# Attention and a mixture of experts in one program: blanking placed by the planner, a second raw buffer at the start, whole-chunk scores for the first pair, and the early expert's first layer beside the last pair

## The chip, the cores and the metric

The program runs on one core of one Trainium2 chip, in one launch. The metric is the device time of an execution in microseconds (us). The kernel before took 1047.83 us in the median of 3 runs (1040.9 to 1049.94).

## The reference

Two stages follow each other. The first is attention with a threshold, for 8 batches (B) of 8 heads (H), 576 positions (S) and 64 channels (D):

```python
scores = scale * np.matmul(q, k.transpose(0, 1, 3, 2))
thresh = np.max(scores, axis=-1, keepdims=True) - tau
scores = np.where(scores >= thresh, scores, -1000000000.0)
scores = scores - np.max(scores, axis=-1, keepdims=True)
attn = np.exp(scores)
attn = attn / (np.sum(attn, axis=-1, keepdims=True) + 1e-09)
return np.matmul(attn, v).astype(np.float32)
```

The second takes the result as 4608 tokens of 512 values and sends each token to one of 8 experts (512 to 1024 to 512):

```python
do_compute = x @ w_skip > 0                 # a token may be skipped: out = x
e_idx = np.argmax(xc @ w_gate, axis=1)      # gate_w is its softmax weight
h = np.maximum(xc[mask] @ w1[e], 0.0)
out = xc + gate_w[mask, None] * (h @ w2[e])
```

## The kernel before, in words

**Pairs and chunks.** The attention is cut into 32 pairs of heads (`g`, four to a batch). The 576 positions are four blocks of 128 and a tail of 64; the tails of a pair's two heads share one block, so a pair has nine chunks (`STEP = 9`): four for each head and one for both tails. Float32 values are split in a high part (`h`) and the rest (`l`), and products are made of the parts.

For each pair `plan_pair` loads q and k as `raw` (128 x 1152 values), casts them to the high part (`hi`, one cast on VectorE or ScalarE) and makes the rest in two halves (`lo`, one for q and one for k, on VectorE or GpSimd). `plan_dist` writes the parts by DMA into a large buffer QK (three transfers of 64 x 1152 values for each head, three buffers in a ring, pair `g` in buffer `g % 3`), and copies two rows of zeros (`zd`, in DRAM) into it; `plan_blk` fills the block BD for the tails. `plan_score` multiplies a chunk's 128 queries with all 576 keys, in two halves of 288 that each have a PSUM buffer (`shp`), and VectorE takes the maximum of each half (`mx`). Once a pair's 18 maxima are there, `plan_thresh` works out the thresholds on VectorE (`mm`, then three steps on `gps`, then `nh` in two parts), PE transposes them to rows (`plan_trow`, L667), and ScalarE puts these into QK. `plan_weights` then multiplies again, now with the threshold subtracted by the product itself (L565, PSUM `sps`), ScalarE exponentiates (`e`, L711), VectorE masks (`p`, L716), `p` is split into fp16 parts (`phh` on ScalarE or VectorE, `phl` on GpSimd, L753), and `plan_av` multiplies with v (L784). v is loaded once for a batch in four transfers of 384 KB (`plan_v`, L459).

**Experts.** After each batch the tokens' logits are computed (`plan_logits`, and `plan_tails` for the tails), `plan_gate` picks experts and slots in lists on VectorE, and GpSimd scatters records to these lists in DRAM (L1134). When seven batches are through, the fullest expert is picked and its first 256 tokens are worked on while the last pairs of the attention still run (`plan_pick`, `plan_early`: its weights are split in high and low parts, `wl` at L1278; its first layer's products are at L1331, with the hidden values in the buffers QK0 and QK1). When all slots are known, the experts' lists are loaded and sorted by size, and eight experts are worked through, of each `layer1`, then `layer2` (L1602).

**What sets the order.** Nothing of the attention is written in the order in which it runs. Each step is an operation of a plan, with the engines that may take it and an estimated cost, the operations it needs, the ring buffer it takes, and a due time: `k` or `n` counts chunks, and the table `OFF` shifts each kind of step against it. `Plan.run` walks forward in its own estimated time, and gives each engine the due operation that can start first. So a changed entry of `OFF` or a new operation moves others, and can move them to another engine. Engines that issue in this fixed order wait on semaphores; SP issues all plain loads and stores in one queue. Before the plan begins, a stretch of plain code sets up constants: GpSimd writes zeros, ones and -1 into the QK, BD, V and `nh` buffers (L274 to L294) and builds index tables, all of it ahead of its first planned operation. A warm-up of 10 products (`WARM`) runs on PE.

Of the kernel before, what the change touches and what calls it, by code (L numbers as in the profile page):

```python
# [62 lines left out]
XW = -7.2  # L63
VS = -2.6
V2 = 60.3
GS = 0.12
DU = 5
WRB = 4
LOOK = 0.1
WARM = 10  # L70
# [6 lines left out]
    ld=19.0, hl=-60.5, hlD=97.9, loD=230.0, di=17.3, S=-15.2, mx=6.5, th=-131.9, tr=-4.4, tc=-40.8, T=-11.5, e=-54.1, p=-11.3, ph=1.9, phD=16.2, pl=0.0, av=4.0, ldv=18.9, v=-11.2, v0=0.0, fmA=4.0, ld0=0.0, init=39.5, row=10.6, dh=21.2, bd=10.6, rsp=-1.6, vsp=49.0, L1=24.0, sc=0.0,  # L77
# [102 lines left out]
def attn_moe_kernel(ctx: ExitStack, tc: tile.TileContext, qk, vl, tau, wg, w1, w2, out):  # L180
# [24 lines left out]
    iod = cp.tile([P, E], F32, name="iod")
    nc.vector.tensor_scalar(iod, ioe, -1.0, float(E - 1), op0=ALU.mult, op1=ALU.add)
    capc = cp.tile([P, 2, E], F32, name="capc")
    for i, cap in enumerate(CAPS):
        nc.gpsimd.memset(capc[:, 0, i : i + 1], float(cap))
        nc.gpsimd.memset(capc[:, 1, i : i + 1], float(cap // P))  # L210
    eoff = cp.tile([P, E], F32, name="eoff")
    nc.vector.tensor_scalar(eoff, ioe, float(NTOK), None, op0=ALU.mult)
    tokp = cp.tile([P, NTP], F32, name="tokp")
    for i in range(2):
        nc.gpsimd.iota(
            tokp[:, i * NM : (i + 1) * NM],
            [[P, NM]],
            base=i * S,
            channel_multiplier=1,
            allow_small_or_imprecise_dtypes=True,  # L220
        )
# [53 lines left out]
    for i in range(QB):  # L275
# [5 lines left out]
        if i == QB - 1:  # L281
            break
# [670 lines left out]
    def plan_tails(b, k, xtm):  # L953
# [31 lines left out]
        if b == B - 1:  # L985
            plan_gate(k + 2, pr, 2 * NM, 1, [y])
# [891 lines left out]
```

## Time and profile before

| what | before |
| --- | --- |
| median of 3 runs | 1047.83 us |
| the profiled execution | 1047.14 us |
| its span (first to last instruction of the profile) | 1045.2 us |
| VectorE busy, instructions | 790.9 us, 1747 |
| TensorE (PE) busy, products | 903.1 us, 9592 |
| ScalarE (ACT) busy | 586.9 us |
| GpSimd (POOL) busy | 685.1 us |
| mean granted clock of TensorE | 0.928 |

Times in a view count from the start of the span. A row of the timeline has the start, the duration, the engine, the line of the kernel, the operation, output <- inputs, the shape, the count of instructions that it groups, and in brackets the idle time ahead of it with what ended that. A row of the groups has line, engine, operation, count, then busy time in us, mean ns of one, and the idle time of the engine before them by what ended it. A row of the windows has the stretch, then for PE, its weight loads, VectorE, ScalarE and GpSimd the busy time and instructions, then the granted clock, the share of the DMA engines and GB/s. SPq stands for DMA issues on SP. The chain that ended last has only its last operations in this profile, so the stages are read from the windows and the timeline.

### The profile page before, as it was taken

To read this page: it belongs to the slowest core of one execution; us is meant where nothing else is said; L and a number is where in the kernel's file an instruction comes from. 1 tells how busy PE (TensorE), PEld (TensorE's weight loads), DVE (VectorE), ACT (ScalarE), POOL (GpSimd) and SP (SyncE) were. 2 spreads that over 40 slices of the span, in tenths; PEclk is the share of its full clock that TensorE was granted. 3 is DMA by queue.
4 is the path that set the end of the run, shared out by engine and by line. 5 is a ranking of instruction groups with operands and counts; after the bars stand their busy time and mean duration, and the time that the engine had idled before them with its cause. 6 is when DMAs were issued, how large, how long until landed. Compare 5 with 4: busy or idle time off the path is not lost. (4 is left out here: it accounts for less than half of the span.)

```text
span 1045.2 us, 24717 instructions
## 1 busy us (share of the span) xinstructions
PE 903.1 (86%) x9592; PEld 833.4 (80%) x9592; DVE 790.9 (76%) x1747; ACT 586.9 (56%) x856; POOL 685.1 (66%) x444
## 2 busy tenths in 40 slices
PE   1888998998799898788899969885787999999995
PEld 1568887987788798688888969875786989999994
DVE  2678988899989689999879989997653455547771
ACT  0356886785577586557768647755441434434450
POOL 6338796796887678688768877957634446544561
PEclk6599999999999899989989989997788999999998
DMA  3976558649447765845865775471234655444530
GB/s 98 243 165 145 132 116 249 145 103 263 109 109 201 191 137 120 236 116 119 212 154 123 199 185 126 86 219 32 82 101 140 213 181 172 130 168 164 193 131 17
DMA packets 81814, 157.39 MB, mean 151 GB/s; under 512 B 28631, under 2 KB 28887, under 8 KB 81696
## 3 DMA queue, kind: packets, MB, share of 16 engines
q1 hardware_dynamic: 77008, 145.51, 53.0%
q0 software_dynamic: 4544, 10.28, 3.0%
q8 instruction: 77, 1.26, 0.5%
q14 instruction: 41, 0.34, 0.1%
q10 hardware_dynamic: 144, 0.00, 0.0%
HBM read 70.80 MB, written 24.78 MB: 91 GB/s over the span
## 5 line engine op out<-in xcount | busy, mean ns | idle before, releaser
L753 POOL TENSOR_TENSOR phl<-p,phh 128x1152 f16<-128x1152 f32 x128 | 310.2, 2426 | 110.3 <-ACT phh L328 89.2
L596 DVE TENSOR_REDUCE mx<-shp 128x1 f32<-128x288 f32 x576 | 245.8, 447 | 45.3 <-PE shp L591 44.0
L591 PE MATMUL shp<-QK 128*128 128x288 f32 x1024 | 225.1, 330 | 47.4 <-DVE mx L596 30.0
L711 ACT ACTIVATE e<-sps,ntau 128x576 f32<-128x576 f32 x288 | 207.1, 736 | 90.9 <-PE sps L565 75.1
L716 DVE SCALAR_TENSOR_TENSOR p<-sps,e 128x576 f32<-128x576 f32 x288 | 214.8, 749 | 36.6 <-ACT e L711 26.9
L591 PEld LDWEIGHTS shp<-QK 128*128 128x128 f32 x1024 | 163.3, 201 | 65.2 <-DVE mx L596 50.7
L565 PE MATMUL sps<-QK 128*128 128x288 f32 x1024 | 192.1, 318 | 17.9 <-DVE p L716 15.0
L565 PEld LDWEIGHTS sps<-QK 128*128 128x128 f32 x1024 | 152.9, 199 | 25.8 <-DVE p L716 18.2
L328 ACT ACTIVATE phh<-p 128x1152 f16<-128x1152 f32 x111 | 128.8, 1161 | 52.0 <-DVE p L716 32.8
L784 PE MATMUL avp<-Vh,phl 128*128 128x65 f16 x1280 | 140.4, 200 | 9.3 <-POOL phl L753 9.2
L780 PE MATMUL avp<-Vh,phh 128*128 128x65 f16 x1280 | 142.6, 202 | 0.5 <-ACT a L328 0.5
L783 PE MATMUL avp<-Vl,phh 128*128 128x64 f16 x1280 | 141.0, 199 | 0.0
L784 PEld LDWEIGHTS <-phl 128*128 128x128 f16 x1280 | 123.8, 102 | 9.9 <-POOL phl L753 9.8
L780 PEld LDWEIGHTS <-phh 128*128 128x128 f16 x1280 | 122.6, 102 | 9.2
L783 PEld LDWEIGHTS <-phh 128*128 128x128 f16 x1280 | 124.0, 103 | 0.7 <-issue 0.6
L1531 POOL TENSOR_TENSOR wl<-wr,wh 128x1024 fp32r<-128x1024 f32 x28 | 72.3, 2599 | 34.7 <-ACT wh L1530 29.4
L1568 PE MATMUL hps<-xh,wl 128*128 128x256 f32 (+4 forms) x256 | 76.7, 300 | 0.0
L1568 PE MATMUL hps<-xh,wh 128*128 128x256 f32 (+4 forms) x248 | 76.2, 307 | 0.1
L1568 PE MATMUL hps<-xl,wh 128*128 128x256 f32 (+4 forms) x248 | 74.8, 301 | 0.0
L1580 POOL DMA_INDIRECT out<-o,ids x21 | 21.1, 1003 | 71.7 <-DVE o L1579 30.1
L1569 ACT ACTIVATE QK<-hps 128x256 fp32r<-128x256 f32 (+4 forms) x64 | 27.0, 422 | 68.3 <-PE hps L1568 67.7
L381 POOL TENSOR_TENSOR hl<-raw,hl 128x576 fp32r<-128x576 f32 x31 | 44.3, 1430 | 30.6 <-ACT vmx L516 16.8
(243 smaller groups left out, 1988.7 us busy)
## 6 DMA issues: line engine op xcount, KB each, us to landing
QK<-hl SPq DMA_DIRECT2D x192, 288.0 KB
wr<-in_w SPq DMA_DIRECT2D x32, 1024.0 KB
raw<-in_qk SPq DMA_DIRECT2D x32, 576.0 KB
vraw<-in_vl SPq DMA_DIRECT2D x32, 384.0 KB
out<-xb SPq DMA_DIRECT2D x32, 256.0 KB
xs<-xb SPq DMA_DIRECT2D x32, 256.0 KB
BD<-hl SPq DMA_DIRECT2D x64, 64.0 KB
QK<-zd SPq DMA_DIRECT2D x64, 4.5 KB
```

What stands on the lines that cost most here:

```text
L328: nc.scalar.activation(dst, src, AF.Copy)
L565: nc.tensor.matmul(ps[:, j, 0:HS], w_, x_[:, js], start=(i == 0), stop=(i == len(mm) - 1))
L591: nc.tensor.matmul(ps[:, 0:HS], w_, x_[:, js], start=(q == 0), stop=(q == len(mm) - 1))
L596: nc.vector.tensor_reduce(T["mx", g][:, o, j : j + 1], T.pop(("S", g, i, j))[:, 0:HS], AX.X, ALU.max)
L711: nc.scalar.activation(e, T["W", g, i][:, :, 0:HS], AF.Exp, bias=ntau, scale=0.125)
L716: nc.vector.scalar_tensor_tensor(T[z][:, kt % 2].rearrange("p (a b) -> p a b", a=2), T.pop(("W", g, i))[:, :, 0:HS], 0.0, T.pop(("e", g, i ...
L753: nc.gpsimd.tensor_tensor(T["pl", g, i], T.pop(z)[:, 0:nk], T["ph", g, i], op=ALU.subtract)
L780: nc.tensor.matmul(pv[:, c, :], x, Vh[:, hd, kt, :], start=(j + q + c == 0), stop=False, skip_group_check=True)
L783: nc.tensor.matmul(pv[:, c, 0:D], x, Vl[:, hd, kt, :], start=False, stop=False, skip_group_check=True)
L784: nc.tensor.matmul(pv[:, c, :], y, Vh[:, hd, kt, :], start=False, stop=(c == NM), skip_group_check=True)
L1531: lo[q % 2].tensor_tensor(w[1][:, sl], rs, w[0][:, sl].bitcast(F32), op=ALU.subtract)
L1568: nc.tensor.matmul(hp_[:, 0:cap], w_, x, start=(i == 0), stop=(i == len(mm) - 1))
```

## The change

1. **The plan's numbers.** Most entries of `OFF` change, with `XW`, `VS`, `V2` and `DU`; the plan's estimate for a DMA of QK rises from 0.82 to 1.08, for a load of raw from 1.64 to 2.17 and of v from 1.1 to 1.44. `WARM` goes from 10 to 24.
2. **Blanking.** Of the plain code ahead of the plan only what pair 0 and pair 1 need is left: VectorE blanks QK1, GpSimd writes its rows of -1, BD0, `nh`, `jt`, then QK2 and BD1. The rest (`settle_a` to `settle_e`: the ones in V, the blanks of QK0, the tables, `seg`) become operations of the plan, due later. Pair `g` now uses QK buffer `(g + 1) % 3`. The copies of zero rows into QK are made only from the fourth pair on, and `zd` is filled later, from a small tile of its own.
3. **Loads at the start.** Pair 1's raw values have a buffer of their own (in the ring `xb`), so their load no longer waits for pair 0's parts. The first loads of v now wait until SP has issued the second head's transfers of pair 0.
4. **Whole chunks.** The scores of pair 0 go into a whole `sps` buffer, and VectorE takes both halves' maxima of a chunk in one instruction.
5. **The early expert.** Its second half of w1 has a buffer in `xb`. Its transposes and first-layer products use the `shp` buffers in place of `sps`, and the buffers QK0 and QK1, which the last pair no longer occupies.
6. **One last gate.** For the last batch, tails and main tokens are transposed into `sps` buffers one after the other, and one gate of five columns takes the place of two gates with one and four.

```diff
+    for h in range(2):
+        blank_qk(nc.vector, 1, h)
+        minus_qk(1, h)
+    nc.gpsimd.memset(BDs[0].bitcast(F32), 0.0)
+    nc.gpsimd.memset(nhs[0].bitcast(F32), 0.0)
...
-        QK, BD = QKs[g % QB], BDs[g % 2]
+        QK, BD = QKs[(g + 1) % QB], BDs[g % 2]
...
+            if g == 1:
+                T["raw", g] = ap_.tile([P, 2 * S], F32, name="raw1", tag="xb")
...
-        mine = [pl.dma(k - OFF["di"] + OFF["dh"] * h - 0.1, zero, ring.take(f"QK{h}", QB), [0.05])]
+        mine = [pl.dma(kd - 0.1, zero, qr + [T["init"]], [0.05])] if g >= QB else []
...
+        def both():
+            T["S", g, i, 0] = ps = sps()
+            for j in range(2):
+                score(j, ps[:, j])
...
+            nc.vector.tensor_reduce(T["mx", g][:, o, :], T.pop(("S", g, i, 0))[:, :, 0:HS], AX.X, ALU.max)
...
-            if b >= B - 2:
-                plan_gate(k + 2, pr, (b % 2) * NM, NM, [y])
+            elif last:
+                plan_gate(k + 2, pr, NM, NM + 1, [y, T["lgt", pr]])
...
-        if b == B - 1:
-            plan_gate(k + 2, pr, 2 * NM, 1, [y])
...
-        x = pl.op(k2, xt, gs + ring.take("sps", SPB), {PE: 0.108 * NDT * jt})
+            t = pl.op(k2 + a, lambda a=a: xt(a), gs + ring.take("shp", SHB), {PE: 0.108 * 2 * jt})
...
+    settle = [
+        pl.op(-40, settle_a, T["start"][1], {DVE: 1.6}),
+        pl.op(62, settle_c, T["start"][1], {POOL: 1.3}),
+        pl.op(64, lambda: settle_b(0), T["start"][1], {POOL: 1.7}),
+        pl.op(65, lambda: settle_b(1), T["start"][1], {POOL: 1.7}),
+        pl.op(70, settle_d, T["start"][1], {POOL: 1.4}),
+    ]
```

What the new numbers and operations do to the order is seen on three queues. A number behind a name tells buffers apart. First SP, from its first load on; `in_qk` and `in_vl` are the inputs in DRAM. Before, where QK_156 is pair 0's buffer:

```order
L360 DMA raw<-in_qk 128x1152
L297 DMA zd<-nh_185 128x9 [waits Pool_49]
L427 DMA QK_156<-zd 2x576 [waits DMAHW2_49]
...
L459 DMA vraw<-in_vl 128x768
...
L1419 TENSOR_LOAD tneg [waits DVE_49]
...
L436 DMA QK_156<-hl 64x2x576 [waits DMAHW5_49,DVE_49]
L438 DMA QK_156<-hl 64x1152 [waits DMAHW6_49,DVE_49]
L440 DMA QK_156<-hl 64x2x576 [waits DMAHW7_49,Pool_49]
...
L360 DMA raw<-in_qk 128x1152 [waits DMAHW2_49]
```

Now, where QK_115 is pair 0's buffer and raw_191 the buffer of pair 1:

```order
L382 DMA raw<-in_qk 128x1152
L1475 TENSOR_LOAD tneg [waits DVE_49]
...
L382 DMA raw_191<-in_qk 128x1152
L461 DMA QK_115<-hl 64x2x576 [waits DVE_49]
L463 DMA QK_115<-hl 64x1152 [waits DVE_49]
L465 DMA QK_115<-hl 64x2x576 [waits Pool_49]
...
L484 DMA vraw<-in_vl 128x768 [waits DMAHW1_49]
...
L437 DMA BD_117<-hl 64x4x64 [waits DMAHW5_49]
...
L461 DMA QK_116<-hl 64x2x576 [waits DMAHW7_49,Activation_49]
...
L382 DMA raw<-in_qk 128x1152 [waits DMAHW2_49]
```

The zero rows and the four loads of v stood ahead of pair 0's parts and now stand elsewhere or behind; pair 1's load moved ahead of them, and the last row, the load of pair 2, stands behind v, BD and half of pair 1's parts.

Second VectorE, from the last maximum of pair 0 to the end of its thresholds (`mm` to `nh`). Before:

```order
L624 TENSOR_REDUCE mm<-mx 128x9 [waits DVE_49]
L628 TENSOR_SCALAR gps<-mm 128x9 [waits DVE_49,Activation_49]
L596 TENSOR_REDUCE mx<-shp 128x1 [waits PE_49]
L632 SCALAR_TENSOR_TENSOR gps<-mm,gps 128x9 [waits DVE_49]
...
L636 SCALAR_TENSOR_TENSOR gps<-mm,tau_123,gps 128x9 [waits DVE_49]
...
L644 CAST nh_185<-gps 128x5 [waits DVE_49,Pool_49]
```

Now:

```order
L668 TENSOR_REDUCE mm<-mx 128x9 [waits DVE_49]
...
L622 TENSOR_REDUCE mx<-shp 128x1 [waits PE_49] x2
L348 CAST hl<-raw 128x2x576 [waits DMAHW2_49]
L672 TENSOR_SCALAR gps<-mm 128x9 [waits Activation_49]
L622 TENSOR_REDUCE mx<-shp 128x1 [waits PE_49]
L676 SCALAR_TENSOR_TENSOR gps<-mm,gps 128x9 [waits DVE_49]
```

The cast of pair 2's high part (L348), which waits for its raw load, now stands between the first and the second link of pair 0's threshold chain.

Third PE, at the end of the attention; `x` and `xb` are the last batch's tails and main tokens, `wgt` the gate's weights, and `tri` the product in each gate that ranks tokens. Before:

```order
L887 MATMUL gps<-ident,x_10811 128x128 x4
...
L1331 MATMUL sps<-QK_156,wl_12898 128x256
...
L1075 MATMUL gps<-rs_13241,tri_74 128x8
...
L887 MATMUL gps<-ident,xb 128x128 x4
L912 MATMUL gps<-wgt,xf 128x16 x4
L1075 LDWEIGHTS tri_74
L1075 MATMUL gps<-rs_13327,tri_74 128x8
...
L1602 MATMUL yps<-wh,QK_156 128x512
```

Now:

```order
L1387 MATMUL shp<-QK_114,wl_12610 128x256
L929 MATMUL sps<-ident,x_10699 128x128 x4
L929 MATMUL sps<-ident,xb 128x128 x4
L1018 MATMUL sps<-wgt,xf 128x16 x2
L955 MATMUL sps<-wgt,xf 128x16 x2
...
L1120 MATMUL gps<-rs_13281,tri_140 128x8
...
L1668 MATMUL yps<-wh,QK_114 128x512
```

The two gates have become one, with both transposes directly ahead of it. Before, 84 of the first layer's 96 products stood behind the last product of the attention; now 36 do, and 48 more than before stand ahead of it.

More of the change, by code (lines that the diff above doesn't have):

```diff
@@ L398, in plan_pair @@
         ]
-        ring.free("raw", [a] + c)
+        ring.free("xb" if g == 1 else "raw", [a] + c)
         T["lo", g] = c
@@ L468, in plan_v @@
                     lambda i=i: load(i),
-                    [(y,) for y in lds[-1:]] or ring.take("vraw", 1) + ring.take("V", 2) + T["start"][0],
-                    [1.1],
+                    [(y,) for y in lds[-1:]] or ring.take("vraw", 1) + ring.take("V", 2) + T["start"][1],
+                    [1.44],
                     0.46,
@@ L598, in plan_score, with tops @@
         deps = [T["bd", g]] if M else T["qk", g, h]
-        for j in range(2):
+        wide = g == 0
+        def both():
+            T["S", g, i, 0] = ps = sps()
+            for j in range(2):
+                score(j, ps[:, j])
+        def tops():
+            if i == 0:
+                T["mx", g] = ap_.tile([P, STEP, 2], F32, name="mx", tag="mx")
+            nc.vector.tensor_reduce(T["mx", g][:, o, :], T.pop(("S", g, i, 0))[:, :, 0:HS], AX.X, ALU.max)
+        if wide:
+            s = pl.op(n + OFF["S"], both, deps + ring.take("sps", SPB), {PE: 0.86 if M else 0.57})
+            m = pl.op(n + OFF["mx"], tops, [s] + (ring.take("mx", 2) if i == 0 else T["mxo", g][0:1]), {DVE: 0.75})
+            ring.free("sps", [m])
+            T.setdefault(("Sop", g, h), []).append(s)
+            T.setdefault(("mxo", g), []).append(m)
+        for j in range(0 if wide else 2):
             s = pl.op(
@@ L891, in ev @@
             copy(e, xf, T.pop(("X", key)))
-        t = pl.op(k, tr, deps + ring.take("gps", 1), {PE: 0.434})
+        t = pl.op(k, tr, deps + (ring.take("sps", SPB) if last else ring.take("gps", 1)), {PE: 0.434})
         x = pl.op(k + 0.3, ev, [t] + ring.take("xf", 2), {ACT: 0.478})
-        ring.free("gps", [x])
+        if not last:
+            ring.free("gps", [x])
         return t, x
@@ L983, in plan_tails @@
         T["lgt", pr] = y = pl.op(k + 1.8, lg, js + [T["lgo", b - 1]], {DVE: 0.1})
-        ring.free("gps", [y])
-        if b == B - 1:
-            plan_gate(k + 2, pr, 2 * NM, 1, [y])
+        ring.free("sps" if last else "gps", [y])
     cnt_op = []
@@ L1110, in plan_gate @@
         gs = GS if pr < B // 2 - 1 else 0.5
-        o = pl.op(k, alloc, deps + ring.take("gate", 2), {DVE: 0.1})
+        o = pl.op(k, alloc, deps + T["settle"] + ring.take("gate", 2), {DVE: 0.1})
         o = x = pl.op(k + gs, a1_, [o] + ring.take("ca", 1), {DVE: 0.2})
@@ L1147, in plan_gate @@
         ring.free("gate", scs)
[L1148 removed]
+        if t0 + nt == NTP:
             ring.free("lg", [o])
@@ L1338, in plan_early @@
                         mm,
-                        [x] + hs + ls + (ring.take("sps", SPB) if i == 0 else mms),
+                        xo[-2:] + hs + ls + (ring.take("shp", SHB) if i == 0 else mms),
                         {PE: 12 * 0.109},
@@ L1358, in plan_early @@
             y = pl.op(k2 + 1.7 + f2, hl, [y], {DVE: 0.66})
-            ring.free("sps", [y])
+            ring.free("shp", [y])
             T.setdefault("L1", []).append(y)
```

284 lines of the change are left out of this document (154 added, 130 removed).

## The prediction

> **What bounds the kernel now.** I read the page first (span, engine shares, slices), then the windows of the first 50 us and the timeline there, then the timeline from 715 us to 803 us, and last the groups of instructions between 60 and 700 us. The page:
>
> ```profile
> span 1045.2 us, 24717 instructions
> PE 903.1 (86%) x9592; PEld 833.4 (80%) x9592; DVE 790.9 (76%) x1747; ACT 586.9 (56%) x856; POOL 685.1 (66%) x444
> DVE  2678988899989689999879989997653455547771
> ```
>
> The span lies 1.94 us under its execution (1047.14 us), which is 0.7 us under the median of the runs shown (1047.83 us); I sum against 1047.14. VectorE's slices (tenths, 26 us each) run at eight and nine for most of the attention, but the first three, 2, 6 and 7, are thin: there the kernel waits for a chain, not for an engine. The windows, whose last column is what the DMA engines moved in GB/s, and the timeline of the start:
>
> ```profile
> 20.00:25.00 5.00, 0.00 (x0) 0.00 (x0) 1.75 (x1) 0.00 (x0) 0.00 (x0) 0.50 0.97 340
> 25.00:30.00 5.00, 0.95 (x2) 0.36 (x2) 2.47 (x5) 0.00 (x0) 0.00 (x0) 0.50 1.06 204
> 30.00:35.00 5.00, 4.79 (x15) 3.71 (x15) 3.04 (x8) 2.09 (x4) 0.84 (x1) 0.50 1.00 255
> 35.00:40.00 5.00, 3.46 (x11) 2.55 (x11) 3.75 (x7) 4.96 (x4) 1.91 (x2) 0.50 1.16 236
> 40.00:45.00 5.00, 4.86 (x18) 3.81 (x16) 3.02 (x7) 0.00 (x0) 4.64 (x2) 0.50 0.97 238
> ```
>
> ```profile
> 0.74 0.40 SPq L360 DMA_DIRECT2D raw<-in_qk  x1
> ...
> 2.54 1.05 POOL L278 MEMSET QK<- 64x1152 f32 x1
> ...
> 3.93 0.57 POOL L279 MEMSET QK<- 2x576 f32 x1
> ...
> 5.45 0.52 POOL L284 MEMSET BD<- 128x512 f32 x1
> ...
> 7.45 0.76 DVE L381 TENSOR_TENSOR hl<-raw,hl 128x576 fp32r<-128x576 f32 x1
> ...
> 15.88 1.40 POOL L381 TENSOR_TENSOR hl<-raw,hl 128x576 fp32r<-128x576 f32 x1
> ...
> 18.93 1.79 SPq L459 DMA_DIRECT2D vraw<-in_vl  x4
> ...
> 23.45 0.96 SPq L440 DMA_DIRECT2D QK<-hl  x1
> ...
> 30.07 2.46 PE L591 MATMUL shp<-QK 128*128 128x288 f32 x7 [0.50 <-DMA QK<-hl]
> ...
> 43.81 0.46 DVE L596 TENSOR_REDUCE mx<-shp 128x1 f32<-128x288 f32 x1 [0.26 <-PE shp L591]
> ...
> 45.86 0.17 DVE L628 TENSOR_SCALAR gps<-mm 128x9 f32<-128x9 f32 x1
> ...
> 50.85 0.41 PE L667 MATMUL sps<-ident,nh 128*34 128x128 f32 x1
> ```
>
> The reader should see: GpSimd blanks buffers until 15.88 us and only then computes one of the two low halves of pair 0, though VectorE had the other at 7.45 us. SP sends that half at 23.45 us, behind four loads of v, and PE has its first full score at 30.07 us, released by that DMA. The maxima of pair 0 end at 44.27 us, the threshold chain starts at 45.86 us, and PE transposes its rows at 50.85 us; the first weights follow. All later pairs follow from there at VectorE's pace. The other end:
>
> ```profile
> 721.55 6.21 DVE L1278 TENSOR_TENSOR wl<-wr,wh 128x512 fp32r<-128x512 f32 x1
> ...
> 778.52 0.19 DVE L1010 TENSOR_REDUCE gw<-lg 128x4 f32<-128x32 f32 x1
> ...
> 782.49 0.16 DVE L1106 SCALAR_TENSOR_TENSOR si<-si 128x4 int32<-128x4 int32 x1
> ```
>
> ```profile
> 787.36 0.97 POOL L1134 DMA_INDIRECT lst<-rec,si  x1 [0.30 <-issue]
> 788.64 0.97 POOL L1134 DMA_INDIRECT lst<-rec,si  x1 [0.30 <-issue]
> ```
>
> ```profile
> 728.56 0.40 PE L667 MATMUL sps<-ident,nh 128*34 128x128 f32 x1 [5.03 <-DVE nh L648]
> ...
> 729.67 1.31 PE L565 MATMUL sps<-QK 128*128 128x288 f32 x4
> ...
> 762.74 0.40 PE L1331 MATMUL sps<-QK,wh 128*128 128x256 f32 x2
> ...
> 763.10 0.40 PE L1331 MATMUL sps<-QK,w 128*128 128x256 f32 x2
> ...
> 764.34 0.19 PE L784 MATMUL avp<-Vh,phl 128*128 128x65 f16 x1
> ...
> 775.83 0.60 PE L887 MATMUL gps<-ident,xb 128*128 128x128 f32 x4
> ```
>
> ```profile
> sum 40.00, PE 33.77 PEld 31.91 DVE 20.93 ACT 18.60 POOL 24.65; mean PE 8.44 PEld 7.98 DVE 5.23 ACT 4.65 POOL 6.16
> ```
>
> A subtraction of the early expert took 6.21 us on VectorE between links of the last pair's threshold chain, and PE idled 5.03 us before its rows. The last product of the attention starts at 764.34 us; two gates follow, the last one's slots are ready at 782.65 us, and their scatters leave GpSimd 1.28 us apart.
>
> **The change, part by part.** *Start.* GpSimd now has, ahead of pair 0's low half, two QK halves at 1.05, four rows of -1 at 0.57, two BD at 0.52 and five smaller fills, which I allow 1.5 together: 6.9 us from its start at 0.73, so 7.6. It also waits for VectorE to blank QK1; at GpSimd's own 1.05 per half that adds under 1 us. VectorE's own queue is then waiting for tau, so this is hidden. The half ends near 9.5 us (9 to 10.5) instead of 17.28, and SP can send it then, 14 us earlier, since no zero rows and no v stand before it. What stands before it is pair 1's load, 576 KB against 1536 KB of v. Before, from that issue to the score took 6.6 us; with two fifths of the bytes ahead I take 4.5 (3 to 6.6): the first full score at 14 us (12 to 17).
>
> Nine whole chunks replace 18 halves. The trace has no 2x288 maximum; it lies between one half (0.46) and two (0.92). Four products took 1.31 us in the row at 729.67, two PSUM buffers overlap them with the maximum, and so 1.1 a chunk (0.8 to 1.3): the last maximum ends near 25 us. On that, the chain would save 19 us. But the order puts a wait ahead of its second link: the cast of pair 2, which needs pair 2's load. Behind it on VectorE stand the threshold chain and pair 1's maxima; PE waits for both. By the order, pair 1's load, pair 0's spread (1728 KB), v, BD, half of pair 1's spread and that load go first, 5.4 MB. The windows from 20 to 45 us moved 255 GB/s in the mean: 21 us from about 8, so it lands at 29, the cast ends at 30, and with the 5.0 us of the old chain (45.86 to 50.85) the rows come at 35.5 us. Ends: 31 us if nothing waits (25 plus the old 6.6), 39 if the DMA runs at the 204 of the slowest row. I take **15 us** off (12 to 19). The blanking that moved behind (QK0, the tables, seg) falls on GpSimd between 9.5 and 25 us, where it had nothing but stood idle before; if that cover were gone it would cost its few us there.
>
> *One last gate.* Before, from the last product (764.34) to the slots (782.65) took 18.3 us. Now 36 products of the early layer follow the last product, three in 0.36 us by the rows at 762.74 and 763.10: 4.3. Then both transposes together, 0.6 more than the 2.69 from 775.83 to the gate, and another 1.1 for the second eviction and its products: 4.4. Then the gate, 4.13 (778.52 to 782.65). Sum 12.8, 5.5 less; a fifth scatter in the last batch gives back 1.28. I take **4 us** off (0 to 6). SP's list load waits for these scatters and the next expert's gather for that; the products of the early second layer, which cover a part, start earlier with the gate.
>
> *Beside the last pair.* QK0 and QK1 are now free when the last pair starts, so 48 more products stand ahead of its last one, 5.7 us at the same price. In the four windows of 10 us from 730 us PE is idle 6.23 of 40, so most hide; I take **+1.5** (0 to 5.7). The last pair's rows now stand behind three more chunks in PE's order; that can cover the 5.03 us of idle time, but the splits still stand in the chain: **3 us** off (0 to 5).
>
> *The body.* The order moves eight low halves from GpSimd to VectorE, three casts of hl from ScalarE to VectorE, and two of phh and six of tph from VectorE to ScalarE:
>
> ```profile
> L381 DVE TENSOR_TENSOR hl<-raw,hl 128x576 fp32r<-128x576 f32 x30 | 40.6, 1353 | 0.0
> L330 DVE CAST hl<-raw 128x1152 fp32r<-128x1152 f32 x22 | 35.7, 1625 | 8.7 <-DMA QK<-hl 2.9 <-PE sps L565 2.8 <-PE sps L671 1.9
> L330 DVE CAST phh<-p 128x1152 f16<-128x1152 f32 x12 | 17.2, 1434 | 0.1
> ...
> L330 DVE CAST tph<-p 128x576 f16<-128x576 f32 x10 | 9.4, 939 | 0.0
> ```
>
> ```profile
> L753 POOL TENSOR_TENSOR phl<-p,phh 128x1152 f16<-128x1152 f32 x118 | 286.0, 2427 | 100.5 <-ACT phh L328 87.0 <-PE avp L784 4.0 <-DMA QK<-hl 3.0
> ...
> L381 POOL TENSOR_TENSOR hl<-raw,hl 128x576 fp32r<-128x576 f32 x28 | 40.0, 1431 | 11.3 <-ACT hl L328 5.5 <-DMA BD<-hl 2.4 <-DVE hl L330 2.1
> ```
>
> VectorE: 8 x 1.353 + 3 x 1.625 - 2 x 1.434 - 6 x 0.939 = 7.2 us more. GpSimd: 8 x 1.431 = 11.4 less. The ends are +7 and -11; VectorE is the fuller engine, but not full, so **+3**. ScalarE has room (56%).
>
> VectorE's low half took 0.76 at 7.45 us, beside fills only, and 1.353 in the mean, beside GpSimd's subtractions. The Trainium skill, SBUF — State Buffer, "Who interferes with whom", says that a VectorE operation with two SBUF inputs blocks for the whole of a GpSimd operation that reads SBUF. The trace agrees in the row of 6.21 us. By that rule at its worst each of the eight waits out one phl (2.43) on top of 0.76: 25.5 instead of 10.8, and the sum would be 15 higher.
>
> Sum: -15 - 4 + 1.5 - 3 + 3 = -17.5, so 1047.1 becomes **1029.5 us**; I say 1029. The new raw buffers and the PSUM rings cost nothing of their own: what they hide behind is in the terms above.
>
> **Rivals.** (1) *The start gives back half.* The pair-2 load, or the scores of pair 1 behind it, come later than 29 us: the row at 39 and a first body that starts short of data. For it: the windows at 20 to 45 us show the DMA engines full. Against: the same bytes moved then too. Gain 7 instead of 15: 1037.
>
> (2) *VectorE waits behind GpSimd in the body.* Eight more two-input operations, each behind a phl: 14.7 us more: 1044, which is no change. For it: the 6.21. Against: GpSimd does 11 us less reading.
>
> (3) *The body gains.* GpSimd's 11.4 us count in place of VectorE's 7.2, since phl releases p's buffers and the products: 1029 - 14 = 1015. For it: phl has the longest total on GpSimd. Against: it waited 87 us for ScalarE's phh.
>
> (4) *Slower.* The eight moved low halves and seven early splits on VectorE meet GpSimd in unbroken runs, as at 721.55 us, where one waited through three operations. Each such meeting costs 6.21 - 1.36 = 4.85 us of every engine behind VectorE. All 15: 1029 + 73 = 1102 us; from six of them on (29 us) it is slower than before by 1%. Against: 30 low halves averaged 1.353, so such runs were rare.
>
> **How the numbers follow.** 1% of this kernel, 10.5 us, is about what a measurement tells from no change; faster means below 1037. Forecast 0.62 (its own terms give 1017 to 1040, mostly below 1037), rival 1 0.12, rival 2 0.09, rival 3 0.13, rival 4 0.04. Faster: 0.62 + 0.13, and a good half of rival 1, less the forecast's upper edge: 0.80. Same: 0.16. Slower: 0.04. The range runs from rival 3 to near rival 2: 1013 to 1042 us.
>
> **What would show it.** Right: PE's first score near 14 us and its rows of pair 0 near 35 us instead of 50.85; a wait of VectorE's cast of hl for the raw load shortly before; PE's idle time before the last pair's rows under 2 us; 13 us from the last product to the slots; a body, from the first to the last masked chunk, within 7 us of before. Wrong: rows of pair 0 after 42 us, low halves on VectorE above 2 us in the mean, a body longer by over 10 us, or an early layer that delays the last product by its whole 5.7 us.

## The result and the profile after

The changed kernel took 1013.87 us in the median of four runs (1009.31 to 1023.03), the kernel before 1048.57 in the same comparison: a ratio of 0.9695, 95% interval 0.9612 to 0.9777. That is 34.7 us less, where the forecast was 18 less. It is faster, as forecast, and it lies 0.87 us inside the range's lower end.

The profiled execution of the changed kernel took 1009.31 us, the fastest of the four. Its page, with the shares of the span and VectorE's 40 slices:

```profile
span 1007.3 us, 24694 instructions
...
PE 897.3 (89%) x9618; PEld 831.1 (83%) x9618; DVE 799.1 (79%) x1727; ACT 591.3 (59%) x863; POOL 667.7 (66%) x426
...
DVE  6799999989898999989899998988643555557771
```

The span is 37.9 us shorter than before (1045.2). VectorE's first three slices read 6, 7, 9 and not 2, 6, 7. Its busy time is 8.2 us longer (799.1 against 790.9): what went away is time in which it waited.

To see where, I count VectorE's masks of chunks (`p`, 288 in all, nine for each pair). A row of this view has the minimum, median and maximum in ns, then the start of the first and of the last instruction, for all masks up to a time. The 36th is the last of the fourth pair, the 270th the last of the thirtieth. Before:

```profile
L716 DVE SCALAR_TENSOR_TENSOR p<-sps,e x36: 734/749/760, 54.8 to 140.3; 128x576 f32<-128x576 f32 x36
...
L716 DVE SCALAR_TENSOR_TENSOR p<-sps,e x270: 695/748/760, 54.8 to 708.2; 128x576 f32<-128x576 f32 x135
...
L716 DVE SCALAR_TENSOR_TENSOR p<-sps,e x288: 695/748/760, 54.8 to 758.4; 128x576 f32<-128x576 f32 x144
```

After:

```profile
L760 DVE SCALAR_TENSOR_TENSOR p<-sps,e x36: 739/749/759, 43.1 to 121.2; 128x576 f32<-128x576 f32 x36
...
L760 DVE SCALAR_TENSOR_TENSOR p<-sps,e x270: 728/752/759, 43.1 to 681.2; 128x576 f32<-128x576 f32 x135
...
L760 DVE SCALAR_TENSOR_TENSOR p<-sps,e x288: 704/751/759, 43.1 to 723.6; 128x576 f32<-128x576 f32 x144
```

The differences of the last columns cut the attention in stretches. The last slot of the experts' lists is ready at 782.65 us before and 744.21 after (744.05 + 0.16, below).

| stretch | before | after | less |
| --- | --- | --- | --- |
| start to the 36th mask | 140.3 | 121.2 | 19.1 |
| 36th to 270th (the body) | 567.9 | 560.0 | 7.9 |
| 270th to 288th (the last two pairs) | 50.2 | 42.4 | 7.8 |
| 288th to the last slot | 24.25 | 20.61 | 3.6 |
| last slot to the end | 262.55 | 263.09 | -0.5 |

The start of the changed kernel, in the timeline:

```profile
9.41 1.43 POOL L403 TENSOR_TENSOR hl<-raw,hl 128x576 fp32r<-128x576 f32 x1
...
10.87 0.62 SPq L465 DMA_DIRECT2D QK<-hl  x1
...
14.43 3.88 PE L617 MATMUL sps<-QK 128*128 128x288 f32 x15 [1.60 <-DMA QK<-hl]
...
22.84 1.22 SPq L382 DMA_DIRECT2D raw<-in_qk  x1
...
26.77 1.78 PE L617 MATMUL sps<-hl,BD 128*128 128x288 f32 x6 [5.14 <-DMA BD<-hl]
...
28.59 0.76 DVE L635 TENSOR_REDUCE mx<-sps 128x2 f32<-128x576 f32 x1 [0.73 <-PE sps L617]
...
33.64 0.75 DVE L348 CAST hl<-raw 128x1152 fp32r<-128x1152 f32 x1
...
33.84 0.17 ACT L542 ACTIVATE vmx<-gps 128x1 f32<-128x1 f32 x1
...
34.30 0.16 DVE L672 TENSOR_SCALAR gps<-mm 128x9 f32<-128x9 f32 x1
...
37.59 0.41 PE L711 MATMUL sps<-ident,nh 128*34 128x128 f32 x1
```

GpSimd's low half starts at 9.41 us and not at 15.88, and ends at 10.84 and not at 17.28. SP sends it at 10.87 us and not at 23.45. PE's first full stretch of scores starts at 14.43 us and not at 30.07. Then PE waits 5.14 us for the block BD, the tails' chunk, whose maximum comes at 28.59 us. Pair 2's values, sent for at 22.84 us, are cast at 33.64 us. The threshold chain's second link starts at 34.30 us, and pair 0's rows are transposed at 37.59 us, 13.3 us earlier than before (50.85).

The end of the attention, first on VectorE, then on PE, where the two lines are the transposes of the last pair's rows and the last product of the attention:

```profile
680.80 0.17 DVE L668 TENSOR_REDUCE mm<-mx 128x9 f32<-128x18 f32 x1
...
683.31 0.16 DVE L676 SCALAR_TENSOR_TENSOR gps<-mm,gps 128x9 f32<-128x9 f32 x1
...
687.99 0.76 DVE L760 SCALAR_TENSOR_TENSOR p<-sps,e 128x576 f32<-128x576 f32 x1 [4.53 <-POOL phl L797]
...
688.67 0.22 DVE L680 SCALAR_TENSOR_TENSOR gps<-mm,tau,gps 128x9 f32<-128x9 f32 x1
...
744.05 0.16 DVE L1151 SCALAR_TENSOR_TENSOR si<-si 128x5 int32<-128x5 int32 x1
```

```profile
696.89 0.27 PE L711 MATMUL sps<-ident,nh 128*34 128x128 f32 x1
...
731.85 0.19 PE L828 MATMUL avp<-Vh,phl 128*128 128x65 f16 x1
```

VectorE now waits 4.53 us in the middle of the last pair's threshold chain, between 683.31 and 688.67 us: the mask ahead of the third link needs a buffer of `p` that GpSimd's `phl` holds. PE waits 1.68 us for a mask up to 695.73 us, then has a chunk of scores, and transposes the rows at 696.89 without a further wait. From the last product (731.85) to the last slot are 12.4 us; before, it was 18.3.

### The profile page after: what moved, and what is told of

The parts are those of the page before. It is cut to its first block, busy times and chain, and to the rows that moved or that the text cites. A ratio compares the mean times of both kernels' runs of the same rounds, so it can differ in the third digit from the quotient of the medians.

```text
span 1007.3 us, 24694 instructions
## 1 busy us (share of the span) xinstructions
PE 897.3 (89%) x9618; PEld 831.1 (83%) x9618; DVE 799.1 (79%) x1727; ACT 591.3 (59%) x863; POOL 667.7 (66%) x426
## 5 line engine op out<-in xcount | busy, mean ns | idle before, releaser
L755 ACT ACTIVATE e<-sps,ntau 128x576 f32<-128x576 f32 x288 | 209.3, 738 | 114.3 <-PE sps L590 103.6
L622 DVE TENSOR_REDUCE mx<-shp 128x1 f32<-128x288 f32 x558 | 237.7, 446 | 28.4 <-PE shp L617 26.0
L617 PE MATMUL shp<-QK 128*128 128x288 f32 x992 | 213.9, 326 | 34.9 <-DVE mx L622 26.1
L617 PEld LDWEIGHTS shp<-QK 128*128 128x128 f32 x992 | 155.1, 198 | 48.2 <-DVE mx L622 35.7
L828 PE MATMUL avp<-Vh,phl 128*128 128x65 f16 x1280 | 137.1, 198 | 9.6 <-POOL phl L797 9.6
L824 PE MATMUL avp<-Vh,phh 128*128 128x65 f16 x1280 | 139.5, 200 | 1.9 <-ACT a L346 1.9
L827 PE MATMUL avp<-Vl,phh 128*128 128x64 f16 x1280 | 138.3, 197 | 0.0
L828 PEld LDWEIGHTS <-phl 128*128 128x128 f16 x1280 | 121.6, 100 | 10.9 <-POOL phl L797 10.7
L824 PEld LDWEIGHTS <-phh 128*128 128x128 f16 x1280 | 121.0, 101 | 8.0
L827 PEld LDWEIGHTS <-phh 128*128 128x128 f16 x1280 | 121.9, 102 | 2.4 <-issue 2.2
L1597 POOL TENSOR_TENSOR wl<-wr,wh 128x1024 fp32r<-128x1024 f32 x28 | 72.4, 2601 | 34.7 <-ACT wh L1596 29.4
L403 DVE TENSOR_TENSOR hl<-raw,hl 128x576 fp32r<-128x576 f32 x41 | 61.8, 1507 | 2.1 <-ACT hl L346 2.1
```

Of the source, the lines that this page charges most:

```text
L617: nc.tensor.matmul(ps[:, 0:HS], w_, x_[:, js], start=(q == 0), stop=(q == len(mm) - 1))
L622: nc.vector.tensor_reduce(T["mx", g][:, o, j : j + 1], T.pop(("S", g, i, j))[:, 0:HS], AX.X, ALU.max)
L755: nc.scalar.activation(e, T["W", g, i][:, :, 0:HS], AF.Exp, bias=ntau, scale=0.125)
L824: nc.tensor.matmul(pv[:, c, :], x, Vh[:, hd, kt, :], start=(j + q + c == 0), stop=False, skip_group_check=True)
L827: nc.tensor.matmul(pv[:, c, 0:D], x, Vl[:, hd, kt, :], start=False, stop=False, skip_group_check=True)
L828: nc.tensor.matmul(pv[:, c, :], y, Vh[:, hd, kt, :], start=False, stop=(c == NM), skip_group_check=True)
```

## The experiments

Each kernel ran beside the kernel before on the same chip, and the number in brackets is its time as a share of that, with the 95% interval. The changed kernel has only the four runs above, so its interval, 0.9612 to 0.9777, is wide, and most of the intervals below overlap it. Two theories stood first. **N**: the plan's new numbers made the body shorter. **C**: the code did.

**1. New code, old numbers.**

```diff
-    ld=22.4, hl=-86.6, hlD=127.9, loD=179.6, di=14.3, S=-93.8, ...
+    ld=19.0, hl=-60.5, hlD=97.9, loD=230.0, di=17.3, S=-15.2, ...
```

> The changed kernel with the plan's numbers of before (all of OFF, XW, VS, V2, DU and the three estimates for DMAs); its code, its blanking, its buffers, whole chunks, one last gate and WARM stay new. What is asked: from the first pair's thresholds to the last pair's, the attention became some 18 us shorter, where the prediction had it 0 to 3 longer. Theory N (the numbers): new due times and DMA estimates have the loads and casts stand where data is there, so VectorE waits less at the batches' borders (idle 75.6 us before against 49.2 now between the second and the 31st threshold). Then this kernel's body is as long as before (within 6 us of 624 between these two thresholds), and it takes about 1030 us. Theory C (the code): buffers and freed QK rings do it whatever the numbers; then the body stays near 609 and the time near 1014. Both expect the last gate's gain of about 4 us to stay. The start's gain hangs on both: the old numbers may put pair 1's maxima ahead of pair 0's thresholds; rows of pair 0 between 35 and 50 us.

Measured: 1029.22 us (0.984, 0.9803 to 0.9876).

**2. Old code, new numbers.** The same exchange in the kernel before.

> The kernel before with the plan's numbers of the change (all of OFF, XW, VS, V2, DU and the three estimates for DMAs) and none of its code. Theory N (the numbers): the body shortens by about 15 us, from 624 to near 609 between the second and the 31st threshold, VectorE's idle time there falls from 75.6 to under 60, and the start stays as before (rows of pair 0 near 50 us): 1033 us. Theory C (the code): no change, 1048 us within 1%. Both zero rows and v still stand ahead of pair 0's parts.

Measured: 1048.62 us (0.9997, 0.9965 to 1.0029). The work of the first 100 us tells the kernels apart (columns: PE, weight loads, VectorE, ScalarE, GpSimd, clock, DMA share, GB/s). Before, then after:

```profile
0.00:100.00 100.00, 64.64 (x492) 54.46 (x492) 61.87 (x147) 37.00 (x48) 51.95 (x79) 0.74 0.66 159
```

```profile
0.00:100.00 100.00, 81.36 (x762) 72.32 (x763) 82.90 (x186) 49.80 (x67) 62.12 (x78) 0.90 0.79 189
```

The changed kernel has 762 products done by 100 us, the kernel before 492; the code alone comes to 685, the numbers alone to 552. The 36th mask stands at 121.2, 140.3, 131.9 and 139.4 us, in the same order. Between the second and the 31st threshold, where N and C had put their numbers, the code alone took 631.0 us and the numbers alone 625.1, against 623.8 before and 609.0 after. N wanted 609 of the numbers, C 609 of the code: neither holds as put. (Of the times, N's 1030 for the first kernel and C's 1048 for the second came.) The numbers alone are worth nothing, the code alone 1.6%, both together 3.05%. This fits a new start that only the code makes possible and that only an order made for it uses fully; that reading is argued, not tested by itself. With the old numbers pair 1's maxima stand ahead of pair 0's thresholds, whose last link ran at 48.8 us. From the 36th to the 270th mask they took 566.2 and 572.2 us, which lies inside what one order alone varies by (experiment 5). In the last two pairs the numbers gained more than the code. First the new code alone, then the new numbers alone:

```profile
L760 DVE SCALAR_TENSOR_TENSOR p<-sps,e x270: 732/749/760, 54.4 to 698.1; 128x576 f32<-128x576 f32 x135
...
L760 DVE SCALAR_TENSOR_TENSOR p<-sps,e x288: 732/749/760, 54.4 to 745.7; 128x576 f32<-128x576 f32 x144
```

```profile
L716 DVE SCALAR_TENSOR_TENSOR p<-sps,e x270: 727/750/760, 51.3 to 711.6; 128x576 f32<-128x576 f32 x135
...
L716 DVE SCALAR_TENSOR_TENSOR p<-sps,e x288: 689/750/760, 51.3 to 756.0; 128x576 f32<-128x576 f32 x144
```

The last two pairs take 47.6 us with the code alone, 44.4 with the numbers alone, against 50.2 before and 42.4 after.

**3. Eight low halves back on GpSimd, in the changed kernel's order.**

```diff
-                o.fn(e)
+                o.fn(SWAP.get(o.tag, e))    # ("lo", 3, 1): "POOL", and seven more
```

> The changed kernel in exactly its order, but eight low halves of the body (pairs 3, 6, 7, 10, 17, 18, 25, 26, one each) that the change had moved from GpSimd to VectorE are written on GpSimd again, at the same place of the order. Theory G (rival 3 of the prediction: GpSimd's relief of 11 us is what the body gained): these 11 us and more come back, 1022 to 1026 us. Theory N (the numbers, through data that is there in time): the place of these eight matters little, within 5 us of 1014. The prediction's term for VectorE (eight low halves of 1.35 to 1.6 us saved on the fuller engine) would have 1002 to 1006.

Measured: 1019.54 us (0.974, 0.9716 to 0.9764), between G's times and N's, and in neither. The prediction's own term for VectorE is out: taking these eight off it does not make the kernel faster. Rival 3 of the prediction is not borne out either: the loss is half of what it wants, and the interval overlaps that of the changed kernel. The body is no longer than with the change's own placement (565.7 us; experiment 5 has the others):

```profile
L776 DVE SCALAR_TENSOR_TENSOR p<-sps,e x36: 743/755/758, 41.8 to 122.5; 128x576 f32<-128x576 f32 x36
...
L776 DVE SCALAR_TENSOR_TENSOR p<-sps,e x270: 728/753/760, 41.8 to 688.2; 128x576 f32<-128x576 f32 x135
```

**4. Pair 0 in halves again.**

```diff
-        wide = g == 0
+        wide = False
```

> The changed kernel with pair 0's scores in 18 halves on the shp buffers again, as before, in place of nine whole chunks. Theory D (the start is bound by transfers: the blocks of the tails landed at 26.8 us and pair 2's raw values at 33.6, the cast of which holds the threshold chain): rows of pair 0 stay within 2 us of 37.6 us and the time within 5 of 1014. Rival (the chain of products and maxima binds): 18 halves with 0.46 us of maximum each take 3 to 5 us longer than nine chunks, so the rows come at 41 to 43 us and the time is 1017 to 1019.

Measured: 1016.59 us (0.9699, 0.9668 to 0.973), rows at 36.58 us.

```profile
L760 DVE SCALAR_TENSOR_TENSOR p<-sps,e x36: 741/749/759, 41.7 to 121.7; 128x576 f32<-128x576 f32 x36
```

Theory D holds: the whole chunks move nothing, since the tails' block and pair 2's values come later than either way of taking maxima.

**5. Ten warm-up products.**

```diff
-        for i in range(WARM):
+        for i in range(10):
```

> The changed kernel in exactly its order, with 10 warm-up products on TensorE in place of 24. The 14 products taken out end at 10.2 us in the changed kernel, and the first score waits until 12.4 us for a transfer, so they hide nothing themselves. If the granted clock after them does not depend on them, the time stays at 1014 (within 3). If it does, the first scores run at half the clock, as they did before until 50 us: the four products of a whole chunk then take 2 us and not 1.46, nine chunks 5 us more, and the rows of pair 0 come at up to 42 us: 1014 to 1019. This run is also the nearest to a second look at the changed kernel beside the next three.

Measured: 1020.92 us (0.9734, 0.97 to 0.9769), above both expected times. The start is nearly the same: the granted clock from 15 to 30 us and from 30 to 45 us is 0.81 and 0.62, with 24 products 0.73 and 0.61, and the rows come at 38.01 us. Most of what differs lies behind the start, in an order that is the same instruction by instruction once the warm-up is over:

```profile
L760 DVE SCALAR_TENSOR_TENSOR p<-sps,e x36: 737/750/758, 43.2 to 124.1; 128x576 f32<-128x576 f32 x36
...
L760 DVE SCALAR_TENSOR_TENSOR p<-sps,e x270: 725/750/759, 43.2 to 698.1; 128x576 f32<-128x576 f32 x135
```

This body took 574.0 us, against 560.0 in the changed kernel's profile. Two more of the kernels below have the same VectorE order up to the last pair (6 and 7): their bodies took 563.7 and 565.4. The stretch from 260 to 360 us shows what varies, first in the changed kernel, then in this one:

```profile
260.00:360.00 100.00, 92.46 (x1239) 86.40 (x1238) 92.94 (x213) 78.17 (x110) 77.06 (x42) 1.00 0.69 167
```

```profile
260.00:360.00 100.00, 88.95 (x1084) 82.96 (x1081) 85.82 (x180) 68.86 (x99) 72.03 (x40) 0.91 0.65 150
```

The granted clock was 1.00 in one execution and 0.91 in the other, and 1239 and 1084 products got done. So a body of this order takes 560 to 574 us, mean 565.8, and the 7.9 us that the table above shows for it lie within what one order varies by: before, it was 567.9. Over the whole body the granted clock was 0.96, 0.95, 0.95 and 0.94 for 560.0, 563.7, 565.4 and 574.0 us, but kernel 3 had 0.96 with 565.7 us. So the clock goes with the time only in part, and whether it is the cause of a longer body or follows from PE's waits no run here shows.

**6. Two last gates.**

```diff
-                plan_gate(k + 2, pr, NM, NM + 1, [y, T["lgt", pr]])
+                plan_gate(k + 2, pr, NM, NM, [y])
...
+        if last:
+            plan_gate(k + 2, pr, 2 * NM, 1, [y])
```

> The changed kernel with the last batch's one gate of five columns cut in two again, one for the tails (one column) and one for the main tokens (four); both blocks still go through the sps buffers. The prediction's term: one gate is worth 4 us (0 to 6) from the last product to the slots, so 1018 us. Measured in the profiles of the two kernels: 19.8 us from the last mask to the last slot after, 23.5 before. Rival: the transposes ahead of each other and the buffers did it, and the second gate's 3.9 us of VectorE hide behind PE and ScalarE; then 1014 to 1015.

Measured: 1016.14 us (0.9704, 0.9674 to 0.9734). The last slot:

```profile
L760 DVE SCALAR_TENSOR_TENSOR p<-sps,e x288: 691/750/759, 41.4 to 727.0; 128x576 f32<-128x576 f32 x144
```

```profile
749.81 0.16 DVE L1153 SCALAR_TENSOR_TENSOR si<-si 128x4 int32<-128x4 int32 x1
```

From the 288th mask to the last slot are 23.0 us, against 20.6 with one gate. One gate is worth 2.4 us there; the time agrees with that, and its interval cannot tell it from nothing. It lies between the two expected times.

**7. The first layer held back.**

```diff
-            t = pl.op(k2 + a, lambda a=a: xt(a), gs + ring.take("shp", SHB), ...)
+            t = pl.op(k2 + a, lambda a=a: xt(a), gs + T["P", NG - 1, STEP - 1] + ring.take("shp", SHB), ...)
```

> The changed kernel with the early expert's transposes and first layer held back until the last masked chunk of the last pair is split, so that no product of it stands beside that pair; buffers and all else as changed. The prediction had the early layer beside the last pair as a cost of 1.5 us to the attention, paid back behind it. If those 48 products (5.7 us) hide in PE's idle time, then holding them back puts 5.7 us more behind the last product, of which the last batch's transposes, copies and gate hide a part: 1016 to 1020. If they do not hide, the attention ends earlier by what they cost, and it comes out within 2 of 1014.

Measured: 1008.92 us (0.9639, 0.9595 to 0.9682), 5 us less than the changed kernel, with intervals that overlap, and less than either expected time.

```profile
L760 DVE SCALAR_TENSOR_TENSOR p<-sps,e x270: 725/750/760, 44.1 to 686.2; 128x576 f32<-128x576 f32 x135
...
L760 DVE SCALAR_TENSOR_TENSOR p<-sps,e x288: 691/749/760, 44.1 to 726.4; 128x576 f32<-128x576 f32 x144
```

```profile
744.75 0.16 DVE L1151 SCALAR_TENSOR_TENSOR si<-si 128x5 int32<-128x5 int32 x1
```

The last two pairs take 40.2 us and not 42.4, and from the 288th mask to the last slot it is 18.5 and not 20.6. Between the last product of the attention and the last gate's logits now stand twelve of the first layer's products, not 36, and the other 84 run behind these logits, where the gate and the scatters leave PE idle. So by these profiles the first layer beside the last pair costs some 4 us, and nothing pays it back: the stretch behind the last slot is no longer (262.2 us).

**8. All blanking ahead of the plan.**

```diff
-    settle = [
-        pl.op(-40, settle_a, T["start"][1], {DVE: 1.6}),
...
+    settle_c()
+    settle_b(0)
+    settle_b(1)
+    settle_d()
+    settle_a()
+    settle_e()
+    settle = []
```

> The changed kernel with all its blanking and tables ahead of the plan again, on the same engines (GpSimd: QK0, tables, seg, some 7 us more ahead of pair 0's low half; VectorE: the ones in V and five table operations ahead of pair 0's cast), nothing of it planned. If the start is a chain through GpSimd's low half (the prediction's first step), that half moves from 9.4 to 15 or 17 us, and SP, whose queue waits for it, sends all that follows so much later: rows of pair 0 at 43 to 45 us, 1020 to 1022. Rival: the transfers bind (v, tails, pair 2), the queue catches up, and it costs under 3 us.

Measured: 1022.39 us (0.9759, 0.9726 to 0.9792).

```profile
14.66 1.42 POOL L403 TENSOR_TENSOR hl<-raw,hl 128x576 fp32r<-128x576 f32 x1
...
42.83 0.41 PE L711 MATMUL sps<-ident,nh 128*34 128x128 f32 x1
```

The low half moved by 5.25 us, the rows by 5.24, the time by 8.5. The chain through GpSimd's low half is as the prediction had it.

Three more kernels ask what carries the start. **R**: pair 0's rows, by which the prediction summed it. **W**: the work that VectorE and PE get done ahead, for pairs 1 and 2 too.

**9. v first.**

```diff
-                    ... + ring.take("V", 2) + T["start"][1],
+                    ... + ring.take("V", 2) + T["start"][0],
```

> The changed kernel with the first batch's four loads of v (1536 KB) ahead of pair 1's load and of pair 0's parts again; they wait for nothing but the first load. Theory Q (the order in SP's queue carries the start, as the prediction's first step has it): the parts of pair 0 share the DMA engines with v, the first score moves from 14.4 to about 20 us and the rows of pair 0 from 37.6 to 41 to 43 us: 1018 to 1020 us. Rival B (bytes: all of it has to land before pair 0's weights and pair 2's cast, in whatever order): rows within 2 us of 37.6, and 1014 to 1016.

Measured: 1024.93 us (0.9755, 0.9729 to 0.9781).

```profile
36.60 0.41 PE L711 MATMUL sps<-ident,nh 128*34 128x128 f32 x1
```

```profile
L760 DVE SCALAR_TENSOR_TENSOR p<-sps,e x36: 734/747/758, 41.1 to 131.7; 128x576 f32<-128x576 f32 x36
```

Q missed the rows and B the time: v in front does not delay pair 0's rows at all (36.60 us), but the 36th mask comes 10.5 us later (131.7) and the time is 11 us longer.

**10. One raw buffer.**

```diff
-            if g == 1:
-                T["raw", g] = ap_.tile([P, 2 * S], F32, name="raw1", tag="xb")
-            else:
-                T["raw", g] = ep.tile([P, 2 * S], F32, name="raw", tag="raw")
+            T["raw", g] = ep.tile([P, 2 * S], F32, name="raw", tag="raw")
```

> The changed kernel without the second raw buffer: pair 1's values wait for pair 0's buffer again, and their load falls behind v in SP's queue. Theory W (what the start gains is VectorE's work done ahead: pair 1's maxima and pair 2's cast beside pair 0, and not pair 0's rows alone): the rows of pair 0 come no later than 37.6 us, but the lead over the kernel before, 19 us at the 18th masked chunk, falls by the 5 to 10 us that pair 1's parts come later: 1019 to 1024. Rival R (the rows of pair 0 carry it, as the prediction summed it): rows at or before 37 us, and 1014 or less.

Measured: 1024.6 us (0.9747, 0.9717 to 0.9778). The rows, the cast behind them, the 36th mask and the work done by 100 us:

```profile
32.52 0.37 PE L711 MATMUL sps<-ident,nh 128*34 128x128 f32 x1 [1.77 <-DVE nh L692]
...
36.63 3.00 POOL L567 TENSOR_TENSOR Vl<-vraw,Vh 128x1536 f16<-128x1536 f32 x1 [7.77 <-ACT Vh L564]
...
37.26 2.99 DVE L348 CAST hl<-raw 128x1152 fp32r<-128x1152 f32 x1
```

```profile
L760 DVE SCALAR_TENSOR_TENSOR p<-sps,e x36: 690/748/759, 40.2 to 129.9; 128x576 f32<-128x576 f32 x36
```

```profile
0.00:100.00 100.00, 74.23 (x656) 67.68 (x656) 79.45 (x173) 42.43 (x56) 54.69 (x73) 0.85 0.71 173
```

The rows come 5 us earlier than in the changed kernel (32.52), and the 36th mask 8.7 us later (129.9). R is out. W comes close with its numbers: the lead at the 18th mask fell by 10.0 us (5 to 10 expected), and the time is 0.6 us above W's range; 656 products are done by 100 us, not 762. Ahead of pair 0's first mask VectorE had done 15 halves of pair 1's maxima in the changed kernel, 10 in kernel 9 and 4 here. The plan also drew up another order behind the edit, in kernel 9 as well.

**11. Pair 0's thresholds first.**

```diff
+    first, T["start"] = T["start"], [[], []]
...
     ahead(-1)
+    T["start"] = first
+    plan_v(0)
...
+    T["hi", 2].deps.append((T["tho", 0], False))
```

> The changed kernel with pair 0's thresholds ahead of two things that stand in their way: pair 2's cast, which waits for its load (33.6 us), and the scale of v, which holds the one gps buffer until 34.0 us. The maxima of pair 0 are there at 29.4 us, and five links take 2.6 us: rows at 32 to 33 us in place of 37.6. Theory R (rows carry the start): 4 to 5 us less, 1009 to 1010. Theory W (work ahead and transfers carry it): pair 2's parts come no earlier for it, the lead at the 36th masked chunk stays at 19 to 20 us, and the time at 1014 within 3.

Measured: 1023.81 us (0.9767, 0.9731 to 0.9802).

```profile
33.39 0.42 PE L712 MATMUL sps<-ident,nh 128*34 128x128 f32 x1
...
34.03 0.76 DVE L348 CAST hl<-raw 128x1152 fp32r<-128x1152 f32 x1 [0.63 <-DMA raw<-in_qk]
```

```profile
L761 DVE SCALAR_TENSOR_TENSOR p<-sps,e x36: 734/748/760, 37.3 to 128.9; 128x576 f32<-128x576 f32 x36
```

The rows come 4.2 us earlier, and pair 2's cast is no later than it was (34.03 against 33.64): its load bounds it. The kernel is still 10 us slower, and only 5 halves of pair 1's maxima stand ahead of the first mask. R is out again. W had 1014, and misses too: this edit also put v's scale later, GpSimd splits v at 48.15 us and not at 38.48, and the plan drew up another order behind that. Which of these took the 10 us was not told apart. The granted clock is another candidate: from 45 to 60 us it was 1.00 in the changed kernel and 0.77, 0.84 and 0.66 in kernels 9, 10 and 11. The intervals of these three overlap that of the changed kernel, and that of kernel 5 (0.9734), which has the changed kernel's start; what stands clear of the scatter is their later 36th mask.

**12. Both**: 11 with the edit of 7.

> The kernel with pair 0's thresholds first, and the early expert's first layer held back behind the last pair as well, which took about 5 us off the changed kernel when it was held back alone. If the two add up: 1004 to 1006 by theory R, 1009 by theory W.

Measured: 1017.54 us (0.9697, 0.9669 to 0.9725). Holding the first layer back took 6.3 us off kernel 11, with intervals that don't overlap, and 5 off the changed kernel. Neither expected time was reached, since 11 was a loss. The best kernel of the study is 7: 0.9639 of the kernel before.

```profile
L761 DVE SCALAR_TENSOR_TENSOR p<-sps,e x36: 735/748/758, 35.6 to 134.3; 128x576 f32<-128x576 f32 x36
```

Up to 731 us this kernel has the same order as 11, and its 36th mask stands at 134.3 us where that of 11 stands at 128.9. So one profile places the 36th mask only within some 5 us.

## Why the prediction was right, and where its sum was off

The direction held, and so did the first links of the start: GpSimd freed early, then the transfers, then the scores. The sum fell short by 15 us, and a body that gained (rival 3) is not what filled it. That rival matched the time, 1015, for a reason that experiment 3 does not bear out. The range's lower end, 1013, came from it; the forecast's own terms ended at 1017. So that the time fell inside the range is in part luck.

- **Start, 15 us forecast, 19.1 measured.** The first links came about nearly as forecast: the low half ended at 10.84 us (9.5, at most 10.5), the first score stood at 14.43 (14), and a chunk took 1.2 us (1.1; eight of them from 14.43 to 24.10). Behind that, two errors partly offset each other: the last maximum ended at 29.35 us (25), since BD landed late, and pair 2's cast ended at 34.39 (30); from there to the rows it took 3.2 us (5.5). So the rows at 37.59 (35.5) are nearer than their steps.

  The prediction also read the old chain a little wrong: before, pair 0's last maximum is the first of the two in the row at 44.73 us and ends at 45.19, not at 44.27, and the chain's first link, `mm`, starts at 45.59.

  The failed step is the measure: "the rows come at 35.5 us" was turned into "I take 15 us off" one for one. The rows gained 13.3 us and the 36th mask 19.1. Pair 1's maxima taken ahead of the rows do not make this difference: before, 8 halves of them stood ahead of pair 0's rows, now 9 do. The difference arises between pair 0's first mask and its ninth, 26.1 us before and 18.2 now. VectorE's three longest waits there, before, add up to 5.2 us, and two of them are

```profile
70.37 0.94 DVE L596 TENSOR_REDUCE mx<-shp 128x1 f32<-128x288 f32 x2 [2.12 <-PE shp L591]
...
73.87 0.76 DVE L716 SCALAR_TENSOR_TENSOR p<-sps,e 128x576 f32<-128x576 f32 x1 [2.50 <-ACT e L711]
```

  In the changed kernel no wait of VectorE there is over 0.2 us. Why these waits went was not tested.

  The 36th masks fall in two groups: 120.8 to 124.1 us in the changed kernel and 3 to 7, and 128.4 to 134.3 in 1 and 8 to 12. The times of the first group are 1009 to 1021 us, those of the second 1018 to 1029. Inside a group the 36th mask does not give the order of the times: 12 has the latest, 134.3, and with 1018 the lowest time of its group, since it holds the first layer back.
- **The wait ahead of the second link** was there (cast at 33.64 us, second link at 34.30), but it had a second holder that the prediction did not see: the one gps buffer, which v's scale released after 33.84 us. Kernel 11 took both out of the way and had its rows 4.2 us earlier, but gained no time; since its order also changed behind that, what the wait itself costs stays open.
- **Whole chunks** were not on the path: BD and pair 2's load are later (experiment 4).
- **One last gate**: 12.4 us from the last product to the slots, 12.8 forecast. By itself the gate is worth 2.4 us (experiment 6). What gives the other 3.5 us of the 5.9 was not tried alone; fewer products of the first layer between the two, 36 and not 84, are a candidate, though in 7, with none ahead of the transposes, it took 12.2 us as well.
- **Beside the last pair, +1.5 forecast**: right in sign. With the 36 products that the prediction put into the gate's sum, it costs some 4 us by the profiles against holding the layer back (7), and 6.3 us by the times of 11 and 12.
- **The last pair's stall, 3 us forecast.** The last two pairs gained 7.8 us. The stall did not go: 4.53 us of it stand at another place, on VectorE, and PE's rows are covered as forecast. The numbers alone give 5.8 of the 7.8 (experiment 2). In that kernel and in the changed one the last pair's maxima are done (`mm`) 0.4 us ahead of the 270th mask (680.80 us in the changed kernel); before, `mm` stood at 718.94 us, 10.7 us behind it. But that is not shown to be the cause: in experiment 9 `mm` stands 10.0 us behind the 270th mask, and the last two pairs take 43.0 us all the same. That term was mis-sized.
- **The body, +3 forecast, -7.9 in the profile.** Four executions with this order take 565.8 us in the mean, before took 567.9 in one. That is no change that these runs can tell, so whether the +3 was right stays open. Low halves on VectorE took 1.5 us in the mean, under the bound of 2, so rival 2 did not come:

```profile
L403 DVE TENSOR_TENSOR hl<-raw,hl 128x576 fp32r<-128x576 f32 x41 | 61.8, 1507 | 2.1 <-ACT hl L346 2.1
```

The rule behind that rival (the Trainium skill, SBUF — State Buffer, "Who interferes with whom") is seen in single rows all the same: in experiment 10 a cast that takes 0.75 us elsewhere took 2.99 us at 37.26, until GpSimd's operation of 3.00 us was over. For a cast, which has one input, the page says this only of a mode of VectorE that uses both its ports; that the cast ran in that mode no run here shows.

Left open: what in kernel 11 cost 10 us, why VectorE's waits between pair 0's masks went, and how much of the last two pairs' gain each of the plan's numbers carries. A run with v's scale alone moved was not made.

## What to carry to other kernels

Measure a start by when the steady pace stands (here the 36th of 288 masks), not by the first milestone of the first piece: kernels 9, 10 and 11 reached that milestone 1 to 5 us sooner and had the 36th mask 8 to 11 us later. One profile places that mask only within some 5 us, so smaller differences say nothing. When a plan's numbers and its code change together, try each alone: here one gave 1.6%, the other nothing, and both 3%. And work that is moved into idle time should be compared with leaving it behind the end: here the chain of the gate and the scatters had more idle time to give.

## What the runs showed of the hardware

The granted clock of TensorE differs between executions of one instruction order: it was 1.00 against 0.91 from 260 to 360 us, and the two bodies, 560.0 and 574.0 us, differ by 14 us. That the clock alone made them differ is not shown. Differences of that size between single profiles of this kernel are no evidence for an edit.

Fourteen more warm-up products did not hold the clock up: it fell to 0.61 from 30 to 45 us with 24 products, 0.62 with ten. The Trainium skill (TensorE: Matmul & The Clock Gate, "Part 1: The HAM clock gate") gives full speed after about 3.4 us of sustained work. The traces agree only in part. In the changed kernel the warm-up's products took 421 ns each up to 7.1 us and 275 ns from 7.6 us on, some 5.8 us after the first; in experiment 5 none of the ten, which ran for 4.6 us, got faster. Behind the warm-up the rule did not hold: in the kernel before, PE was busy 4.86 of the 5 us from 40 to 45 us at a granted 0.50.
